# A gated transformer block on one core: a new hand-fixed order, with small operations shared out anew and thirteen more ordering pairs

## The chip, the cores and the metric

The kernel runs on one NeuronCore of one Trainium2 chip. The metric is the device time of one execution in microseconds (us). The engines are TensorE (PE: matmuls, and PEld: the weight loads that overlap them), VectorE (DVE), ScalarE (ACT), GpSimd (POOL) and SyncE (SP), which issues nearly all DMA transfers. Each engine works through its own instruction list strictly in order and waits on semaphores where an operand comes from another engine or from a transfer.

## The reference

One block on a sequence of 2048 tokens with 448 features, in bfloat16: attention in a sliding window and a gated MLP with a spatial product, each behind a layer norm that a conditioning vector modulates.

```python
mod = (silu(c) @ w_mod)                      # six vectors of 448
sa, ca, ga, sb, cb, gb = split(mod)
h = layernorm(x) * (1 + ca) + sa
x = x + ga * A(h)
h = layernorm(x) * (1 + cb) + sb
return x + gb * B(h)

def A(x):                                    # 16 heads of 28
    q, k, v = split(x @ wqkv)
    scores = q @ k.T * 28 ** -0.5
    scores = where(0 <= i - j < 256, scores, -1e9)
    return (softmax(scores) @ v) @ wo

def B(x):                                    # w_in: 448 x 1792
    z = gelu(x @ w_in)
    z1, z2 = z[:, :896], layernorm(z[:, 896:])
    return (z1 * (w_sp @ z2 + b_sp)) @ w_out # w_sp: 2048 x 2048
```

## The kernel before

The kernel is built in two passes. First every operation is recorded with `add`: the engines that may run it, its dependencies, and the buffers or PSUM banks (`take`) that it needs. Each gets a number in the order of recording. Then `order()` walks the words of a string, `ORDER`. A word such as `188.p.0.2` says: operation 188 goes next on PE (p; a is ACT, v DVE, g GpSimd, s SP) and takes options 0 and 2 of its buffers. So the string fixes at once which engine runs an operation, the order within each engine, and which buffers are reused when; a reused buffer adds a dependency on its last readers. A second string, `AFTER`, holds pairs such as `54-368`: operation 368 is to wait for operation 54 as well. `count`, `waits` and `emit` then turn dependencies into semaphore waits and leave out those that an engine's earlier waits already cover. The times that `order()` works out along the way steer nothing here.

The work in the program, in the order of time:

- Start: x comes in as two half blocks (L371: 256 tokens each, 224 KB) and three blocks of 512 tokens (L362, 448 KB each). w_mod and wqkv come in by pieces (L357, L358, L367, L368), wqkv's first into a staging tile `wq_st`, from which small copies (L543, L544) spread the heads into `WQK`. TensorE runs warm-up matmuls (L509) whose results nobody reads.
- Each tile of 128 tokens gets its statistics on DVE (L552, L555, L557, L564; L560 on GpSimd), a norm into `xn` (L572 on DVE, L579 on GpSimd), a transpose on TensorE and an evacuation with the modulation into `hT` (L637 on ACT, L639 on DVE).
- q and k come from `hT` and `WQK` and are evacuated 256 wide (L704 on ACT, L705 on DVE) or 512 wide (L725 on ACT, L726 on DVE) into `qT` and `KT`; v is evacuated into `Vaug` (L756, L757).
- Attention: scores (L827, TensorE), exps on ScalarE straight from PSUM into `PA` (L860 for the main blocks, L892 for the strips beside them), mask products on DVE or GpSimd (L870, L907, L910), weighted sums (L936), the output projection (L959).
- The second norm and `hT`, then z = h @ w_in: the second half z2 by tokens (L1015), with gelu on ScalarE (L1026, L1038), squares for its variance (L1047) and the normalisation on DVE (L1033, L1052) or GpSimd (L1030); the first half z1 by features (L1061).
- The spatial product (L1085) in two halves `wspA` and `wspB` of w_sp, which DMA transposes (L432) bring in transposed; b_sp and the gate (L1089, L1092); the last product (L1104) and the outputs.

Of the kernel before, what the change touches and what calls it, by code (L numbers as in the profile page):

```python
# [22 lines left out]
AFTER = "54-368 469-468 460-563 393-291 447-336 384-282 523-811 329-328 160-49 281-284 401-291 418-129 410-127 414-331 426-431 511-614 510-814 515-811 666-682 822-820 385-284 289-291 821-820"  # L23
# [50 lines left out]
class Sched:  # L74
# [23 lines left out]
    def order(self):  # L98
# [3 lines left out]
        self.prog = {e: [] for e in ENGS}  # L102
        for pair in AFTER.split():
            first, then = pair.split("-")
# [1084 lines left out]
```

## Time and profile before

| what | value |
|---|---|
| time, median of 3 runs | 269.0 us (268.57 to 269.16) |
| the profiled execution's own time | 268.23 us |
| its span in the trace | 266.5 us |
| instructions on PE / DVE / ACT / POOL | 2919 / 358 / 189 / 181 |
| granted TensorE clock | 1.00 throughout |
| HBM read and written | 9.53 MB and 1.84 MB |

The span is that of the one execution which the profiler followed, and 1.73 us of that execution's time lie outside it. The busy time of TensorE in the table of engines includes warm-up matmuls. The share of busy time is an average over stages that have different limits, so the profile is read by stage: the start up to the first exp at 15.97 us, attention up to about 99, z up to 146.07, where the spatial product starts, and from there to the end.

### The profile page before, as it was taken

The numbers are of one execution on the slowest core, as the hardware profiler recorded it, in microseconds if no ns is written. First come the engines' busy times: TensorE is split into PE (matmuls) and PEld (weight loads), VectorE is DVE, ScalarE is ACT, GpSimd is POOL, SyncE is SP. The second block draws the span as 40 slices with busy tenths as digits, with TensorE's granted clock in tenths as the row PEclk, the third lists the DMA queues.
The fourth block names the chain that finished last, engine by engine and source line by source line (L and its number), as shares of the span: only waits on it lengthen the run. The fifth ranks groups of instructions, "written<-read, shape, count | busy, mean of one in ns | idle before, by whom it ended". The sixth has DMA issues, their size and how long they took to land.

```text
span 266.5 us, 6861 instructions
## 1 busy us (share of the span) xinstructions
PE 261.0 (98%) x2919; PEld 136.3 (51%) x2919; DVE 152.5 (57%) x358; ACT 131.0 (49%) x189; POOL 132.6 (50%) x181
## 2 busy tenths in 40 slices
PE   7999999999999999999999999999999999999996
PEld 3764565565577666454444444444444444444454
DVE  6799999999999998887363001112203242033264
ACT  3799899999999995779996400000000000000000
POOL 7656665556599666452876002315604845030430
PEclk9999999999999999999999999999999999999999
DMA  7990425982996646449999994000000000000133
GB/s 221 331 326 16 99 40 81 126 106 44 165 207 81 126 80 91 82 98 183 180 175 194 170 195 114 0 2 0 1 0 2 0 0 0 2 17 0 52 114 95
DMA packets 66297, 25.46 MB, mean 96 GB/s; under 512 B 57813, under 2 KB 65562, under 8 KB 66266
## 3 DMA queue, kind: packets, MB, share of 16 engines
q1 hardware_dynamic: 65848, 24.52, 46.0%
q8 instruction: 23, 0.38, 0.6%
q10 hardware_dynamic: 418, 0.50, 0.5%
q14 instruction: 8, 0.07, 0.1%
HBM read 9.53 MB, written 1.84 MB: 43 GB/s over the span
## 4 chain that ended last, share of the span: by engine, by line
PE 88%; ACT 8%; DVE 2%; POOL 1%; issue 0%; ACTq 0%
PE ps L1085 36%; PE ps L1015 8%; PE ps L1061 8%; PE ps L1104 8%; PE ps L715 5%; ACT PA L860 5%; PE ps L827 5%; PE ps L936 4%; PE ps L752 4%; PE ps L959 3%; PE ps L679 2%; ACT PA L892 2%; PE ps L509 2%; POOL PA L870 1%; POOL rs_all L560 1%; DVE PA L910 0%
## 5 line engine op out<-in xcount | busy, mean ns | idle before, releaser
L1092 POOL TENSOR_TENSOR z1T<-tmpg,z1T 128x512 bf16<-128x512 bf16 x28 | 31.9, 1154 | 73.7 <-DVE tmpg L1089 73.7
L1089 DVE TENSOR_TENSOR tmpg<-ps,bsp_bc 128x512 bf16<-128x512 f32 x28 | 18.8, 689 | 86.7 <-PE ps L1085 59.7
L860 ACT ACTIVATE PA<-ps 128x1536 bf16<-128x1536 f32 (+4 forms) x64 | 60.0, 974 | 1.1 <-PE ps L827 0.4
L1085 PE MATMUL ps<-wspB,z 128*128 128x512 bf16 x224 | 49.8, 379 | 0.0
L1085 PE MATMUL ps<-wspA,z 128*128 128x512 bf16 x224 | 49.3, 379 | 0.0
L1085 PEld LDWEIGHTS ps<-wspA,z 128*128 128x128 bf16 x224 | 21.8, 98 | 26.6 <-issue 0.4
L1085 PEld LDWEIGHTS ps<-wspB,z 128*128 128x128 bf16 x224 | 21.9, 98 | 26.3 <-DVE tmpg L1089 0.2
L936 PEld LDWEIGHTS ps<-Vaug,PA 128*128 128x128 bf16 x720 | 20.9, 96 | 5.2 <-issue 1.6
L560 POOL TENSOR_TENSOR rs_all<-ve_all,neghalf 128x1 f32<-128x1 f32 (+1 forms) x31 | 20.7, 678 | 4.1 <-DVE ve_all L557 3.7
L1015 PE MATMUL ps<-w_in,hT 64*128 64x448 bf16 x224 | 22.7, 349 | 0.0
L936 PE MATMUL ps<-Vaug,PA 128*128 128x32 bf16 x720 | 22.5, 176 | 0.0
L1061 PE MATMUL ps<-hT,w_in 64*128 64x512 bf16 x196 | 22.3, 376 | 0.0
L1104 PE MATMUL ps<-w_out_g,z1T 128*128 128x448 bf16 (+3 forms) x126 | 22.2, 332 | 0.0
L870 POOL TENSOR_TENSOR PA<-PA,mask 128x1024 bf16<-128x1024 bf16 x7 | 15.9, 2274 | 8.5 <-ACT PA L860 2.9
L715 PE MATMUL ps<-hT,WQK 128*128 128x512 bf16 x80 | 20.0, 380 | 0.0
L827 PE MATMUL ps<-qT,KT 32*64 32x64 bf16 (+3 forms) x768 | 18.0, 223 | 1.4 <-ACT PA L860 0.6
L552 DVE BATCH_NORM_STATS2 st_all<-x_sb 128x6 f32<-128x448 bf16 x32 | 19.2, 612 | 0.0
L579 POOL TENSOR_SCALAR xn<-x_sb,rs_all,ve_all 128x448 bf16<-128x448 bf16 x18 | 14.8, 828 | 6.1 <-DVE PA L907 2.1
L892 ACT ACTIVATE PA<-ps 128x1536 bf16<-128x1536 f32 (+1 forms) x16 | 16.4, 1024 | 2.2 <-PE ps L827 2.0
L907 DVE TENSOR_TENSOR PA<-PA,mask 128x2048 bf16<-128x2048 bf16 x14 | 16.9, 1216 | 0.5 <-ACT PA L860 0.3
L1104 PEld LDWEIGHTS ps<-w_out_g,z1T 128*128 128x128 bf16 x126 | 11.7, 98 | 10.1 <-DVE fin L1115 0.2
L1015 PEld LDWEIGHTS ps<-w_in,hT 64*128 64x128 bf16 x224 | 10.8, 94 | 10.7 <-issue 0.4
(114 smaller groups left out, 334.0 us busy)
## 6 DMA issues: line engine op xcount, KB each, us to landing
w_in<-in_B_w_in_dram SPq DMA_DIRECT2D x8, 224.0 KB, 4.0
out_dram<-fin SPq DMA_DIRECT2D x15, 112.0 KB, 1.7
x_sb<-in_A_x_dram SPq DMA_DIRECT2D x3, 448.0 KB, 4.4
wmod<-in_w_mod_dram SPq DMA_DIRECT2D x1, 1344.0 KB, 9.6
w_out_g<-in_B_w_out_dram SPq DMA_DIRECT2D x1, 784.0 KB, 6.2
wq_st<-in_A_wqkv_dram SPq DMA_DIRECT2D x3, 224.0 KB, 4.6
bsp_bc<-in_B_b_sp_dram SPq DMA_DIRECT2D x1, 512.0 KB, 5.1
x_sb<-in_A_x_dram SPq DMA_DIRECT2D x2, 224.0 KB, 3.6
```

The lines of the kernel that those rows point to most:

```text
L552: st = [dve(0.62 if True else 0, lambda e, t=t, ci=ci, s=s: e.bn_stats(st_all[:, slot, t, ci, :], s()), deps(t), prio) for ci, s in enumer ...
L560: rs = pool(0.41 + 0.155 * len(tiles), lambda e: e.tensor_tensor(rs_all[:, slot, a:b], ve_all[:, slot, a:b], neghalf[:, 0:b - a], ALU.pow) ...
L715: m = pe(4 * MMS, [lambda e, h=h, g=g, kc=kc, tb=tb: e.matmul(ps[:, h.slot[0], :], lhsT=WQK[:, kc, 4 * g:4 * g + 4, :].rearrange("p a b -> ...
L827: return [lambda e, t=t: e.matmul(to(t), lhsT=KT[32 * t:32 * t + 32, qi, key:key + kn], rhs=qT[32 * t:32 * t + 32, qi, q0:q0 + qn], start= ...
L860: return e.activation(cols(place(kb, hf) + 64 + 768 * a, [[384, 2 * (b - a)], [1, w]]), ps[:, h.slot[0]:h.slot[0] + b - a, 2 * n * w:(2 * ...
L892: return e.activation(cols(EXTRAS[ext[n].slot[0]] + 128 * a, [[128, b - a], [512, 4], [1, 128]]), ps[:, h.slot[0]:h.slot[0] + b - a, :].re ...
L936: fns.append(lambda e, hO=hO, hd=hd, bi=bi, kb=kb, nb=nb, j=j, c=(2 * t + k) * 384 + 128 * (j - kb), half=half: e.matmul(ps[:, hO.slot[0], ...
L1015: return lambda e, kc, p0, start, stop: e.matmul(ps[:, hs[t % 2].slot[hf], 0:D], lhsT=hT[p0:p0 + 64, kc, t * 128:(t + 1) * 128], rhs=w_in[ ...
L1061: return lambda e, kc, p0, start, stop: e.matmul(ps[:, hs[b // 2].slot[b % 2], :], lhsT=w_in[p0:p0 + 64, kc, ft * 128:(ft + 1) * 128], rhs ...
L1085: m = pe(16 * MMS, [lambda e, h=h, si=si, ft=ft, tb=tb: e.matmul(ps[:, h.slot[0], :], lhsT=z2[:, si, ft * 128:(ft + 1) * 128], rhs=(wspA i ...
L1092: u = pool(1.16, lambda e, ht=ht, ft=ft, tb=tb: e.tensor_tensor(z1T[tb][:, ft, :], tmpg[:, ht.slot[0], :], z1T[tb][:, ft, :], ALU.mult), [ ...
L1104: return [lambda e, ft=ft: e.matmul(ps[:, h.slot[0], c0:c1], lhsT=z1T[t // 4][:, ft, (t % 4) * 128:(t % 4 + 1) * 128], rhs=w_out_g[:, ft, ...
```

## The change

Only the two strings differ. `ORDER` names the same operations in another sequence and puts 84 of them on another engine: DVE has 367 recorded operations after 358, GpSimd 166 after 177, ScalarE 176 after 174; TensorE's 326 and SP's 127 stay the same in number. Small operations (memsets, copies, norms, evacuations) make up most of those that move. `AFTER` has 35 pairs after 22, and the 13 new ones stand at its end. The other pairs are kept.

```diff
 ORDER = """
-2.a 28.v 39.g 0.s 37.g 29.v 30.v 31.v 32.v 58.p.0 40.g 3.a 4.s 43.g ...
+2.a 28.v 37.g 0.s 30.v 35.v 43.g 65.p.0 3.a 4.s 32.v 73.p.0 39.g 67.p.0 ...
 """
-AFTER = "54-368 469-468 ... 289-291 821-820"
+AFTER = "54-368 469-468 ... 289-291 821-820 427-328 477-597 443-338 238-239 380-384 422-331 426-328 464-468 481-564 490-581 632-648 506-814 982-976"
```

The first place is SP's queue at the start. `x_sb` is x in SBUF, `wq_st` the staging tile of wqkv; `128x2x448` is half a block of x and `128x4x448` a whole one. Before, from the third load of SP's queue on:

```order
L368 DMA wq_st<-in_A_wqkv_dram 128x896
L371 DMA x_sb<-in_A_x_dram 128x2x448
L368 DMA wq_st<-in_A_wqkv_dram 128x896 x2
L367 DMA wq_st<-in_A_wqkv_dram 64x896
L362 DMA x_sb<-in_A_x_dram 128x4x448
L358 DMA wo_g<-in_A_wo_dram 64x448
L358 DMA wv<-in_A_wqkv_dram 64x448
L362 DMA x_sb<-in_A_x_dram 128x4x448
```

And after the change, from the same load on:

```order
L368 DMA wq_st<-in_A_wqkv_dram 128x896
L362 DMA x_sb<-in_A_x_dram 128x4x448
L371 DMA x_sb<-in_A_x_dram 128x2x448
L368 DMA wq_st<-in_A_wqkv_dram 128x896 x2
L367 DMA wq_st<-in_A_wqkv_dram 64x896
L362 DMA x_sb<-in_A_x_dram 128x4x448
L357 DMA wv<-in_A_wqkv_dram 128x3x448
L358 DMA wv<-in_A_wqkv_dram 64x448
L358 DMA wmod<-in_w_mod_dram 64x1792
L357 DMA wmod<-in_w_mod_dram 128x3x1792
L432 DMA_TRANSPOSE wspA<-in_B_w_sp_dram 128x1024
L358 DMA wo_g<-in_A_wo_dram 64x448
```

Block 2 of x, which stood as the second `128x4x448` of the first list, now stands ahead of the second half block and of three pieces of wqkv. Block 3, not shown, comes next after the last row, and so behind a DMA transpose of w_sp.

The second place is DVE between the first statistics of the second half block and the first `hT`. `mv_all` and `ve_all` are the means and variances; the `COPY` rows with `wq_st` spread wqkv. Before:

```order
L552 BN_STATS st_all<-x_sb 128x6
L543 COPY WQK<-wq_st 128x16x28
L555 BN_AGGR mv_all<-st_all 128x2
L557 TENSOR_SCALAR ve_all<-mv_all 128x1
L543 COPY WQK<-wq_st 128x16x28 x2
L564 SCALAR_TENSOR_TENSOR ve_all<-mv_all,rs_all 128x1
L449 MEMSET wv 64x224
L572 TENSOR_SCALAR xn<-x_sb,mv_all,rs_all 128x448 x2
L639 TENSOR_SCALAR hT<-ps,modT 128x256 x3
```

After:

```order
L552 BN_STATS st_all<-x_sb 128x6
L555 BN_AGGR mv_all<-st_all 128x2
L543 COPY WQK<-wq_st 128x16x28
L557 TENSOR_SCALAR ve_all<-mv_all 128x1
L543 COPY WQK<-wq_st 128x16x28
L564 SCALAR_TENSOR_TENSOR ve_all<-mv_all,rs_all 128x1
L543 COPY WQK<-wq_st 128x16x28
L572 TENSOR_SCALAR xn<-x_sb,mv_all,rs_all 128x448 x2
L552 BN_STATS st_all<-x_sb 128x6
L705 CAST qT<-ps 128x256
L639 TENSOR_SCALAR hT<-ps,modT 128x256 x2
```

The memset has left this place, the last copy stands behind the small `ve_all` step, and a statistics step and an evacuation of q have moved ahead of `hT`'s.

The third place is ScalarE from its first exp on: `PA` holds the exps, and the other rows are evacuations. Before:

```order
L892 ACTIVATE PA<-ps 128x3x4x128
L892 ACTIVATE PA<-ps 128x4x128
L860 ACTIVATE PA<-ps 128x6x256
L756 ACTIVATE Vaug<-ps 128x16x28
L860 ACTIVATE PA<-ps 128x2x256
L860 ACTIVATE PA<-ps 128x6x256
L704 ACTIVATE KT<-ps 128x256
L860 ACTIVATE PA<-ps 128x2x256
L860 ACTIVATE PA<-ps 128x6x256
```

After:

```order
L892 ACTIVATE PA<-ps 128x3x4x128
L892 ACTIVATE PA<-ps 128x4x128
L860 ACTIVATE PA<-ps 128x6x256
L860 ACTIVATE PA<-ps 128x2x256
L860 ACTIVATE PA<-ps 128x6x256
L756 ACTIVATE Vaug<-ps 128x16x28
L860 ACTIVATE PA<-ps 128x2x256
L860 ACTIVATE PA<-ps 128x6x256
L520 ACTIVATE gg_sb<-ps 128x448
L860 ACTIVATE PA<-ps 128x2x256
L860 ACTIVATE PA<-ps 128x6x256
L725 ACTIVATE qT<-ps 128x512
```

The Vaug evacuation stands later and the KT evacuation has gone to DVE; a 512-wide evacuation of q, which DVE did, has come in.

More of the change, by code (lines that the diff above doesn't have):

```diff
@@ L21 @@
 """
-AFTER = "54-368 469-468 460-563 393-291 447-336 384-282 523-811 329-328 160-49 281-284 401-291 418-129 410-127 414-331 426-431 511-614 510-814 515-811 666-682 822-820 385-284 289-291 821-820"
+AFTER = "54-368 469-468 460-563 393-291 447-336 384-282 523-811 329-328 160-49 281-284 401-291 418-129 410-127 414-331 426-431 511-614 510-814 515-811 666-682 822-820 385-284 289-291 821-820 427-328 477-597 443-338 238-239 380-384 422-331 426-328 464-468 481-564 490-581 632-648 506-814 982-976"
 class Hold:
```

2 lines of the change are left out of this document (1 added, 1 removed).

## The prediction

> **What bounds the kernel now.** I read the page's head and chain first, then busy time in six stretches, then who waits for whom from 15 to 100 us, then single rows.
>
> The first fence holds the head of the page with its chain by engine; then the busy times by stretch (stretch, its length, busy PE, PEld, DVE, ACT, POOL, the granted clock, the DMA share, GB/s); then two groups of the waits between 15 and 100 us (idle us, how many, the longest), and three links of the chain.
>
> ```profile
> span 266.5 us, 6861 instructions
> PE 261.0 (98%) x2919; PEld 136.3 (51%) x2919; DVE 152.5 (57%) x358; ACT 131.0 (49%) x189; POOL 132.6 (50%) x181
> PE 88%; ACT 8%; DVE 2%; POOL 1%; issue 0%; ACTq 0%
> 0.00:15.20 15.20, 13.57 (x121) 8.42 (x122) 11.52 (x39) 9.32 (x21) 9.60 (x25) 1.00 0.91 277
> 15.20:24.00 8.80, 8.29 (x155) 4.94 (x156) 8.31 (x26) 8.37 (x11) 6.80 (x8) 1.00 0.53 191
> 24.00:52.00 28.00, 27.94 (x519) 14.79 (x516) 26.46 (x52) 26.82 (x31) 17.32 (x16) 1.00 0.50 78
> 52.00:99.00 47.00, 46.08 (x1060) 29.65 (x1059) 46.16 (x93) 45.15 (x53) 32.62 (x46) 1.00 0.71 118
> 99.00:146.00 47.00, 47.00 (x509) 23.13 (x506) 31.97 (x106) 38.23 (x70) 29.41 (x55) 1.00 0.78 141
> 146.00:266.50 120.50, 118.09 (x576) 55.41 (x574) 28.13 (x46) 3.13 (x7) 36.81 (x34) 1.00 0.19 43
> PEld ps L827 <- ACT PA L860: 5.7, 15, 0.5
> ACT PA L892 <- PE ps L827: 2.0, 5, 0.7
> 73.91 1.46 ACT PA L860
> 77.36 1.95 ACT PA L860 x2
> 146.07 72.62 PE ps L1085 x336
> ```
>
> TensorE looks like the bound all along, but four regimes lie under its 98%. Up to 15.2 us the DMA is 91% busy: the kernel waits for its loads, and much of TensorE's work there is warm-up matmuls that nobody reads. From 15.2 to 99 TensorE lacks 0.51 + 0.06 + 0.92 = 1.49 us, ScalarE 0.43 + 1.18 + 1.85 = 3.46 and DVE 0.49 + 1.54 + 0.84 = 2.87: three engines full at once, and the chain hops onto ScalarE's exps (L860, L892), whose banks the next scores (L827) wait for. From 99 to 146 TensorE has no idle time at all, and from 146 it streams the spatial product. So a delay put on the first exp, or work added to ScalarE before 99, comes out at the end, less what of those 1.49 us it closes; a delay on GpSimd or DVE behind 99 must first be longer than its cover.
>
> **The start loads.** In SP's queue the 448 KB of x block 2 now stand ahead of the second half of x block 0 and of three pieces of wqkv. The rows are SP's issues (start, length), three landings (KB each, us from issue), the first consumers on DVE, and the first exp on ScalarE.
>
> ```profile
> 3.04 0.43 SPq L371 DMA_DIRECT2D x_sb<-in_A_x_dram  x1
> 3.51 0.94 SPq L368 DMA_DIRECT2D wq_st<-in_A_wqkv_dram  x2
> 4.50 0.47 SPq L367 DMA_DIRECT2D wq_st<-in_A_wqkv_dram  x1
> 6.42 0.38 SPq L362 DMA_DIRECT2D x_sb<-in_A_x_dram  x1
> 10.40 0.49 SPq L362 DMA_DIRECT2D x_sb<-in_A_x_dram  x1
> x_sb<-in_A_x_dram SPq DMA_DIRECT2D x1, 224.0 KB, 4.5
> wq_st<-in_A_wqkv_dram SPq DMA_DIRECT2D x1, 112.0 KB, 4.9
> x_sb<-in_A_x_dram SPq DMA_DIRECT2D x1, 448.0 KB, 4.2
> 7.55 0.63 DVE L552 BATCH_NORM_STATS2 st_all<-x_sb 128x6 f32<-128x448 bf16 x1
> 9.28 0.46 DVE L543 COPY WQK<-wq_st 128x448 bf16<-128x448 bf16 x2
> 9.90 0.24 DVE L449 MEMSET wv<- 64x224 uint32 x1
> 10.18 0.70 DVE L572 TENSOR_SCALAR xn<-x_sb,mv_all,rs_all 128x448 bf16<-128x448 bf16 x2
> 11.38 1.05 DVE L639 TENSOR_SCALAR hT<-ps,modT 128x256 bf16<-128x256 bf16 x3 [0.49 <-PE ps L630]
> 15.97 2.08 ACT L892 ACTIVATE PA<-ps 128x1536 bf16<-128x1536 f32 x2 [0.39 <-PE ps L827]
> ```
>
> The half block, issued at 3.04, lands 4.5 later, at 7.54; DVE's statistics start on it at 7.55. The last wqkv piece lands at 4.50 + 4.9 = 9.40, between the starts of the two copies (9.28 and about 9.5), so the second takes it as it lands; the norms and transposes that lead to the first exp at 15.97 follow without a hole. Loads land in the order of their issue. From 9.40 to the landing of x block 1 at 6.42 + 4.2 = 10.62, 448 KB took 1.2 us while the DMA was 91% busy. Put ahead, block 2 moves everything behind it by that 1.2; with its own issue on SP (0.38 to 0.59 for such loads) partly in front, I take 1.3. Bounds: 0 if other engines of the DMA were free for it, 1.8 if the issue adds in full. The 1.2 is a price of this very transfer at this very place, so I stay close to it.
>
> The Trainium skill's page "DMA: Bandwidth & Descriptors", section "Where 436 GB/s comes from", says that a load from HBM is bound by the core's share of HBM, about 358 GB/s, and not by the 435 of the ports; as estimates 1.28 or 1.05 us for 448 KB, and the term by the one or the other would be that. The rows' 1.2 us (about 380 GB/s) lies between, so this trace does not show the lower figure as a strict limit.
>
> Between statistics and norms a memset (L449, 0.24, with its step 0.28) leaves DVE: −0.25. Two of the warm-up groups that TensorE runs ahead of the modulation go later, but what follows waits for the same loads: 0. A statistics step (0.63) now stands ahead of `hT`'s evacuations, where DVE waited 0.49 for a transpose: 0, and with the small evacuation that comes along up to +0.4. First exp: 1.3 − 0.25 = +1.05.
>
> **ScalarE from 16 to 50 us.** Its rows here, and the mean of the 512-wide evacuation:
>
> ```profile
> 19.28 0.55 ACT L756 ACTIVATE Vaug<-ps 128x448 bf16<-128x448 f32 x1
> 21.51 0.43 ACT L704 ACTIVATE KT<-ps 128x256 bf16<-128x256 f32 x1
> 27.57 2.08 ACT L892 ACTIVATE PA<-ps 128x1536 bf16<-128x1536 f32 x2 [0.67 <-PE ps L827]
> L725 ACT ACTIVATE qT<-ps 128x512 bf16<-128x512 f32 x4 | 2.4, 596 | 0.0
> ```
>
> Between the first and the third main exp a Vaug evacuation (0.55) and a KT evacuation (0.43) leave and one Vaug evacuation (0.55) comes in: −0.43. After that two evacuations of about 0.59 leave and three of 0.60 come, one of them before the 0.67 us in which ScalarE waited at 27.57 for scores: net 1.80 − 1.18 = 0.62 added, 0.67 of it covered: 0. If the cover is gone because the scores are late too, +0.6; if the scores come early, −0.4. From about 50 us to 99 ScalarE's order is unchanged, so it carries its shift on.
>
> **DVE takes over small work.** Rows: GpSimd's and DVE's norm (count, sum, mean ns), and the norms on GpSimd that go over first.
>
> ```profile
> L579 POOL TENSOR_SCALAR xn<-x_sb,rs_all,ve_all 128x448 bf16<-128x448 bf16 x16 | 13.4, 842 | 5.7 <-DVE PA L907 2.1 <-DVE PA L870 1.5 <-DVE PA L910 1.3
> L572 DVE TENSOR_SCALAR xn<-x_sb,mv_all,rs_all 128x448 bf16<-128x448 bf16 x3 | 1.2, 388 | 0.0
> 17.11 2.82 POOL L579 TENSOR_SCALAR xn<-x_sb,rs_all,ve_all 128x448 bf16<-128x448 bf16 x4 [0.30 <-DVE ve_all L564]
> ```
>
> Between 15.2 and 24 three norms come over: 3 × 0.388 = 1.16 us more on an engine with 0.49 idle, so at most 0.67 of delay for the evacuations queued behind them. Each leaves GpSimd 0.84 sooner, which helps the same transposes. Bounds 0 and 0.7; most evacuations there are TensorE's feed one tile ahead, so I take +0.2, nearer to the lower end. Over 24 to 99 some further small operations come, against 2.4 us of idle time: 0, up to +0.5.
>
> The Trainium skill's page "SBUF — State Buffer", section "Who interferes with whom", speaks against such a move: DVE's scalar operations can use the port pair that it shares with GpSimd, and whichever engine issues first keeps the other out for its whole instruction. By it each of the three norms could stand behind one of GpSimd's (0.71), and the term would be up to 0.67 + 2.1; the 388 ns mean on DVE, with GpSimd at work through those stretches, shows no such wait. On GpSimd's side the trace agrees: the same norm takes 0.71 in the four at 17.11 and 0.84 in the mean, the rest of them beside DVE's mask products.
>
> **The seam and the end.** ScalarE's square, GpSimd's last normalized tile before the spatial product, and SP's last transposes of w_sp:
>
> ```profile
> 112.11 1.08 ACT L1047 ACTIVATE fin<-z,mv_all 128x896 bf16<-128x896 bf16 x1
> 143.99 1.09 POOL L1030 TENSOR_SCALAR z<-z,rs_all,ve_all 128x896 bf16<-128x896 bf16 x1
> 142.21 8.95 SPq L432 DMA_TRANSPOSE wspB<-in_B_w_sp_dram  x6
> ```
>
> One gelu that frees banks for the gate's matmuls now stands behind such a square, 1.08 later: the other banks' matmuls lie between, and TensorE has no idle time there to show how many, so +0.1, with bounds from 0 to half a square, 0.5. The last tile of z is ready at 145.08, the spatial product starts at 146.07: 1 us of slack, and the order there brings that tile no later. The last transposes for the first half stand two places sooner. Behind 146 the tables differ little: 0.
>
> **The sum.** 1.05 − 0.43 + 0 + 0.2 + 0.1 = +0.92. The profiled execution took 268.23 (span 266.5 and 1.73 around it), 0.77 under the median of 269.0. I put the shift on the median: 269.9. Its own bounds: start 0.8 to 1.5 in place of 1.05, ScalarE −0.4 to +0.6 about its term, DVE 0 to 0.7, seam 0 to 0.5, which do not all go one way; I take +0.4 to +2.5, 269.4 to 271.5.
>
> **Rivals.**
> Faster (0.22): the start's delay is absorbed. The loads of the early stage have spare places (wmod's large pieces land sooner or later without a reader), the memset and the two warm-up groups go, and the regrouped evacuations close TensorE's waits of 15 to 99 us. These hold 1.49 at most, and half of it with −0.43 and −0.25 is −1.4 at best: 267.6 to 268.4, at its middle 268.0. It decides if the first exp starts at 15.97 or sooner. For it: three engines have their waits at the same places, where small moves pay; against it: 7.55 and 9.40 are starts on the instant of a landing.
>
> Slower by far (0.13): x block 3 stands behind a DMA transpose of w_sp in SP's queue, and more transposes follow it early. It was issued at 10.40, and this row shows when it was first read:
>
> ```profile
> DMA to landing us min/median/max: 2.8/4.4/10.1
> 23.79 0.62 DVE L552 BATCH_NORM_STATS2 st_all<-x_sb 128x6 f32<-128x448 bf16 x1
> ```
>
> The longest landing, 10.1, is this load's: 20.5, so 3.3 us of cover. Transposes go at 8.95 / 6 = 1.5 us each; two of them ahead take 3 us and a third 4.5, and then DVE's in-order queue stands, and evacuations with it: +1 to +2 on top of the forecast, about 272. It decides once block 3 lands after 24.
>
> No change (0.13): block 2's transfer finds gaps (the DMA share is 91%, that is 1.4 us of 15.2 unused), the start loses only 0.3, and the other terms cancel: 268.9.
>
> **How the numbers follow.** Forecast 0.52, of which 0.06 lie within 0.2% (0.54 us, about what a measurement of this kernel can tell from no change). Faster 0.22; same 0.13 + 0.06 = 0.19; slower 0.46 + 0.13 = 0.59. The range leaves out about a tenth at each end: into the faster rival down to 268.2, up to the middle of the far slower one at 272.0.
>
> **What would show it.** In the changed kernel's profile: DVE's first statistics of the second half block at 8.7 to 8.9 in place of 7.55; the last wqkv copy at 10.6 to 10.8; the first L892 row at about 17.0; the ScalarE row at 73.91 about 0.8 later; the first L1085 row at about 147. A first L892 at 16.0 or below refutes the start; L1085 at 147 and an end that is not later by as much refutes the stream; a stall on DVE at L552 around 24 to 27 us is the far slower case.

## The result, and the profile after

The changed kernel took 270.41 us (median of 6 runs, 270.02 to 270.66) where the kernel before, run beside it, took 269.01: a ratio of 1.0051 with a 95% interval of 1.0038 to 1.0064, or +1.40 us. Run a second time on another occasion it took 270.88 beside 268.65, 1.0079 (1.0066 to 1.0092). Forecast were 269.9 and a range of 268.2 to 272.0.

The two traces differ by more than the medians, since the profiled execution of before was 0.77 below its median and that of after (270.52) 0.11 above: span 266.5 against 268.6, +2.1. A shift that is read against the trace of before can therefore be some tenths too large.

The head of the page after, with its chain by engine, and two groups of its waits between 15 and 100 us (idle us, how many, the longest):

```profile
span 268.6 us, 6839 instructions
PE 259.3 (97%) x2898; PEld 135.9 (51%) x2919; DVE 156.5 (58%) x367; ACT 132.1 (49%) x191; POOL 126.1 (47%) x170
PE 74%; ACT 10%; DVE 9%; DMA 2%; issue 1%; SPq 1%
PEld ps L827 <- ACT PA L860: 7.6, 19, 0.6
ACT PA L892 <- PE ps L827: 1.8, 5, 0.4
```

DVE's share of the chain went from 2% to 9%, and transfers are now in it. Where the 2.1 us came in is read by following the same rows down the two traces. SP's start, the first reader of the half block on DVE, and ScalarE's first exp, its next strip exp and the exp that stood at 52.44 before (its row of before is put last):

```profile
3.04 0.45 SPq L362 DMA_DIRECT2D x_sb<-in_A_x_dram  x1
3.53 0.51 SPq L371 DMA_DIRECT2D x_sb<-in_A_x_dram  x1
9.40 0.63 DVE L552 BATCH_NORM_STATS2 st_all<-x_sb 128x6 f32<-128x448 bf16 x1 [1.04 <-DMA x_sb<-in_A_x_dram]
17.61 2.08 ACT L892 ACTIVATE PA<-ps 128x1536 bf16<-128x1536 f32 x2 [0.39 <-PE ps L827]
28.89 2.08 ACT L892 ACTIVATE PA<-ps 128x1536 bf16<-128x1536 f32 x2 [0.29 <-PE ps L827]
53.67 2.08 ACT L892 ACTIVATE PA<-ps 128x1536 bf16<-128x1536 f32 x2 [0.44 <-PE ps L827]
...
52.44 2.08 ACT L892 ACTIVATE PA<-ps 128x1536 bf16<-128x1536 f32 x2 [0.30 <-PE ps L827]
```

The half block is read 1.85 later (9.40 for 7.55), the first exp stands 1.64 later (17.61 for 15.97), and by 53.67 ScalarE has won 0.41 of that back: +1.23. It keeps this until 75 us. Then DVE, GpSimd, TensorE and ScalarE show this (the last row is the kernel before):

```profile
74.06 1.64 DVE L564 SCALAR_TENSOR_TENSOR ve_all<-mv_all,rs_all 128x1 f32<-128x1 f32 x1
73.56 2.12 POOL L870 TENSOR_TENSOR PA<-PA,mask 128x1024 bf16<-128x1024 bf16 x1 [1.82 <-DVE PA L870]
77.01 0.40 PE L827 MATMUL ps<-qT,KT 32*128 32x256 bf16 x8 [0.43 <-DVE ve_all L564]
79.75 0.93 PE L959 MATMUL ps<-wo_g,hT 128*128 128x448 bf16 x4 [0.39 <-DVE ve_all L557]
77.46 4.05 ACT L860 ACTIVATE PA<-ps 128x1536 bf16<-128x1536 f32 x4 [0.34 <-PE ps L827]
81.82 1.45 ACT L860 ACTIVATE PA<-ps 128x1536 bf16<-128x1536 f32 x1 [0.31 <-PE ps L827]
148.35 10.74 PE ps L1085 x49
...
79.83 1.45 ACT L860 ACTIVATE PA<-ps 128x1536 bf16<-128x1536 f32 x1
```

A step on one column of numbers (L564), which takes 0.14 to 0.17 us in 14 of its 17 places in this trace, took 1.64 us: from 74.06 to 75.70, while GpSimd's mask product ran from 73.56 to 75.68. DVE's queue stood behind it, TensorE waited 0.43 and 0.39 for what DVE brought late, and ScalarE's exps after that are about 2.0 late (81.82 for 79.83). This step, operation 596, ran on GpSimd before. On the chain the spatial product begins at 148.35 for 146.07, and the span ends 2.1 later, so nothing more is added behind it.

### The profile page after: what moved, and what is told of

Read it like the earlier page. It is cut to its first block, busy times and chain, and to the rows that moved or that the text cites. A ratio compares the mean times of both kernels' runs of the same rounds, so it can differ in the third digit from the quotient of the medians.

```text
span 268.6 us, 6839 instructions
## 1 busy us (share of the span) xinstructions
PE 259.3 (97%) x2898; PEld 135.9 (51%) x2919; DVE 156.5 (58%) x367; ACT 132.1 (49%) x191; POOL 126.1 (47%) x170
## 4 chain that ended last, share of the span: by engine, by line
PE 74%; ACT 10%; DVE 9%; DMA 2%; issue 1%; SPq 1%
PE ps L1085 36%; PE ps L1015 8%; PE ps L1061 8%; PE ps L1104 8%; ACT PA L860 7%; PE ps L959 3%; PE ps L715 3%; PE ps L827 3%; PE ps L936 3%; ACT PA L892 3%; DMA wq_st<-in_A_wqkv_dram 2%; DVE st_all L552 2%; PE ps L752 2%; DVE PA L907 1%; DVE xn L572 1%
## 5 line engine op out<-in xcount | busy, mean ns | idle before, releaser
L860 ACT ACTIVATE PA<-ps 128x1536 bf16<-128x1536 f32 (+3 forms) x64 | 60.2, 974 | 1.8 <-PE ps L827 0.9
L1085 PE MATMUL ps<-wspB,z 128*128 128x512 bf16 x218 | 49.2, 379 | 0.3
L560 POOL TENSOR_TENSOR rs_all<-ve_all,neghalf 128x1 f32<-128x1 f32 (+1 forms) x31 | 19.8, 639 | 8.3 <-DVE ve_all L557 7.4
L870 POOL TENSOR_TENSOR PA<-PA,mask 128x1024 bf16<-128x1024 bf16 x8 | 18.0, 2247 | 7.3 <-ACT PA L860 3.8
L715 PE MATMUL ps<-hT,WQK 128*128 128x512 bf16 x71 | 17.8, 379 | 1.0 <-ACT PA L860 0.3
L1069 ACT ACTIVATE z1T<-ps 128x512 bf16<-128x512 f32 x28 | 14.8, 607 | 2.3 <-PE ps L1061 2.3
```

Of the source, the lines that this page charges most:

```text
L560: rs = pool(0.41 + 0.155 * len(tiles), lambda e: e.tensor_tensor(rs_all[:, slot, a:b], ve_all[:, slot, a:b], neghalf[:, 0:b - a], ALU.pow) ...
L715: m = pe(4 * MMS, [lambda e, h=h, g=g, kc=kc, tb=tb: e.matmul(ps[:, h.slot[0], :], lhsT=WQK[:, kc, 4 * g:4 * g + 4, :].rearrange("p a b -> ...
L860: return e.activation(cols(place(kb, hf) + 64 + 768 * a, [[384, 2 * (b - a)], [1, w]]), ps[:, h.slot[0]:h.slot[0] + b - a, 2 * n * w:(2 * ...
L1085: m = pe(16 * MMS, [lambda e, h=h, si=si, ft=ft, tb=tb: e.matmul(ps[:, h.slot[0], :], lhsT=z2[:, si, ft * 128:(ft + 1) * 128], rhs=(wspA i ...
```

## The experiments

Each edit moves words of `ORDER`; a number with v, g or s is one operation on DVE, GpSimd or SP. "Before" is always the kernel before, run on the same chip in the same job. The ratio is taken over the executions and need not be the quotient of the two medians.

| run | median us | before us | ratio (95%) | first exp in its trace |
|---|---|---|---|---|
| x2_back | 269.88 | 268.73 | 1.0047 (1.0035 to 1.0059) | 16.91 |
| x2_front | 269.92 | 268.73 | 1.0056 (1.0041 to 1.0071) | 17.45 |
| early_var | 269.89 | 268.73 | 1.0051 (1.0024 to 1.0077) | 17.43 |
| both_mended | 269.32 | 268.73 | 1.0026 (1.0012 to 1.0041) | 17.84 |
| start_whole | 269.95 | 268.65 | 1.0037 (1.0024 to 1.0050) | 16.86 |
| all_mended | 269.29 | 268.65 | 1.0024 (1.0014 to 1.0033) | 17.26 |
| changed_again | 270.88 | 268.65 | 1.0079 (1.0066 to 1.0092) | 17.77 |
| lock_in_before | 270.25 | 268.65 | 1.0059 (1.0043 to 1.0075) | 16.27 |
| start_full | 270.22 | 268.73 | 1.0057 (1.0043 to 1.0071) | 16.96 |
| all_full | 269.50 | 268.73 | 1.0026 (1.0010 to 1.0041) | 16.49 |
| best_try | 269.23 | 268.93 | 1.0012 (0.9997 to 1.0027) | 16.38 |

**The load alone, put into the kernel before.**

```diff
-... 6.s 41.g 62.p.0 47.g 1.s ... 11.s 150.v 73.p.4 163.a 188.p.0.2 164.p.3 15.s ...
+... 6.s 41.g 62.p.0 47.g 15.s 1.s ... 11.s 150.v 73.p.4 163.a 188.p.0.2 164.p.3 ...
```

> The kernel before with one word moved: x block 2's load goes ahead of the second half block, as in the changed kernel. Theory 1: the half block is read 1.8 later, at about 9.4, the first exp at 17.6 to 17.9, and the time rises by 1.5 to 1.9 to 270.5 to 270.9, more than the whole change cost, since the savings of the change on ScalarE are not in it. Theory 2: attention's waits take the delay up, and the time rises by at most 0.5.

DVE's first read of the half block, the first exp, and the exp that stood at 52.44:

```profile
8.82 0.63 DVE L552 BATCH_NORM_STATS2 st_all<-x_sb 128x6 f32<-128x448 bf16 x1 [1.50 <-DMA x_sb<-in_A_x_dram]
17.45 1.45 ACT L892 ACTIVATE PA<-ps 128x1536 bf16<-128x1536 f32 x1 [0.39 <-PE ps L827]
54.05 2.08 ACT L892 ACTIVATE PA<-ps 128x1536 bf16<-128x1536 f32 x2 [0.45 <-PE ps L827]
```

One moved load costs +1.19 us between the medians and, by the ratio of 1.0056 (1.0041 to 1.0071), +1.5 us: four of the six executions lie at 269.8 to 270.0, two at 270.8 to 270.9. Expected were 1.5 to 1.9, with the half block read 1.8 later. The trace shows the mechanism: read 1.27 later, first exp +1.48, and +1.61 at 54.05, so attention took up none of it. It is a control for the forecast's ScalarE term as well: in the order before the delay grows by 0.13 from 16 to 54 us, in the changed order it shrinks by 0.41.

**The load alone, taken back in the changed kernel.**

```diff
-... 15.s 52.a 70.p.1 44.g 68.p.1 139.v 1.s ... 12.s ...
+... 52.a 70.p.1 44.g 68.p.1 139.v 1.s ... 12.s 15.s ...
```

> The changed kernel with one word moved: x block 2's load goes back behind wqkv's pieces and x block 1, as before. Theory 1 (the start's delay reaches the end): the second half block is read at about 7.55 in place of 9.40, the first exp stands at 15.9 to 16.1 in place of 17.61, and the time falls by 1.2 to 1.6, to 268.8 to 269.2. Theory 2 (the start is absorbed, and the loss comes from GpSimd keeping DVE out of its port at 74 to 75.7 and what waits behind it): the exp moves but the end falls by at most 0.4, to 270.0 or more.

```profile
8.20 0.62 DVE L552 BATCH_NORM_STATS2 st_all<-x_sb 128x6 f32<-128x448 bf16 x1
11.82 0.63 DVE L552 BATCH_NORM_STATS2 st_all<-x_sb 128x6 f32<-128x448 bf16 x1 [0.56 <-DMA x_sb<-in_A_x_dram]
16.91 2.08 ACT L892 ACTIVATE PA<-ps 128x1536 bf16<-128x1536 f32 x2 [0.39 <-PE ps L827]
```

The time is 269.88, still 1.15 above the kernel before. The first exp came only 0.70 sooner, and neither theory had that. One reason stands in the second row: in the changed order a statistics step that reads block 2 stands ahead of the evacuations of `hT`, and with the load back behind block 1 DVE waited 0.56 there. The order was made for the early load. The edit had undone one part and made a wait of the other. The 0.70 is itself uncertain: both_mended, below, has the same start, and its first exp stands at 17.84.

**The reader taken back too.** Operation 272 goes behind the statistics of block 1.

```diff
-... 15.s ... 1.s ... 12.s ... 272.v ... 227.v ... 276.v ...
+... 1.s ... 12.s 15.s ... 227.v ... 272.v 276.v ...
```

> The changed kernel with x block 2's load back behind x block 1, and with the one statistics step that reads block 2 (it stood ahead of the evacuations of hT on DVE) put behind the four steps that read block 1. If the first try fell short because that step now waited for block 2 in DVE's queue (0.56 us at 11.82): no wait for block 2 on DVE before 15 us, the first exp at 15.6 to 16.2, and the time 1.3 to 1.8 below the changed kernel on the same chip. If instead the start's delay has another cause in the changed order: first exp still at 16.8 or later and no more than 0.7 gained.

```profile
8.12 0.16 DVE L500 COPY modT<-ps 128x4 f32<-128x4 f32 x1 [1.51 <-PE ps L488]
8.45 0.41 DVE L639 TENSOR_SCALAR hT<-ps,modT 128x256 bf16<-128x256 bf16 x1
8.77 0.62 DVE L552 BATCH_NORM_STATS2 st_all<-x_sb 128x6 f32<-128x448 bf16 x1
16.86 2.08 ACT L892 ACTIVATE PA<-ps 128x1536 bf16<-128x1536 f32 x2 [0.39 <-PE ps L827]
```

The wait for block 2 is gone, but the first exp stays at 16.86, as in the expectation's second branch. The time is 0.93 below that of the changed kernel run beside it (270.88, changed_again), between the two branches. The half block is read at 8.77 although nothing waits for the load any more; DVE is held by the modulation, which TensorE brings at 8.12 (7.28 in the kernel before), and by an evacuation that now stands ahead of the statistics. So a second delay lay behind the first, hidden by the late load. Its size here is partly chance: this execution took 271.07, 1.12 above the median, and with the same order ahead of it the modulation came at 7.54 in x2_back and 8.06 in changed_again.

**The start as a whole.** Statistics (150) ahead of the modulation's copies, and two warm-up groups later.

```diff
-... 59.p.0 ... 61.p.0 ... 55.p.0 ... 112.v 164.p.2 113.v 162.v ... 150.v ... 69.p.1 ...
+... 55.p.0 ... 150.v 112.v 164.p.2 113.v 162.v ... 69.p.1 59.p.1 61.p.1 ...
```

> The changed kernel with block 2's load and its reader put back as in the run before, and two things more: the statistics of the second half block stand ahead of the modulation's copies on DVE (before, they stood right behind them), and two of the seven warm-up groups that TensorE runs ahead of the modulation go behind it. If the changed order is fitted to a late half block and has a second delay behind the first (the statistics started 8.77 with the load there at 7.51, since DVE held the modulation, 8.12, and an evacuation ahead of it): the statistics start at 7.5 to 7.6, the first exp at 15.6 to 16.1, and the time falls by 0.6 to 1.2 below the run before, to 0 to 0.5 above the kernel before (the port's lock is still in it). If the delay behind the loads is a third thing: first exp still after 16.5.

This run settles less than it was made for. The statistics start on the landing, but that came late in the traced execution, at 7.94, and the first exp stood at 16.96, beyond the 16.5 that the expectation named for a third cause; the time, 270.22, is no lower than that of start_whole, where 0.6 to 1.2 less was expected. With the same start the next run (all_full) read the half block at 7.47 and had its first exp at 16.49:

```profile
7.94 0.63 DVE L552 BATCH_NORM_STATS2 st_all<-x_sb 128x6 f32<-128x448 bf16 x1 [1.33 <-DMA x_sb<-in_A_x_dram]
...
7.47 0.63 DVE L552 BATCH_NORM_STATS2 st_all<-x_sb 128x6 f32<-128x448 bf16 x1 [0.86 <-DMA x_sb<-in_A_x_dram]
```

In all_full the norms that follow start at 10.06, 0.12 sooner than in the kernel before (10.18), and yet the first exp is 0.52 later. The transposes of these norms stand at 11.47 on TensorE, for 10.94 before, right behind 13 matmuls for q and k. So what is left of the start's loss in all_full comes in on TensorE, between the norms and their transposes.

**The port's lock.** This is the stall at 74.06, laid to the port pair that DVE shares with GpSimd. The step moves three places ahead in DVE's queue, so that it comes before GpSimd's product:

```diff
-... 469.v ... 464.v ... 627.v 345.v 468.g ... 596.v ...
+... 469.v ... 596.v 464.v ... 627.v 345.v 468.g ...
```

> The changed kernel with one small step of DVE (the variance step of L564 that took 1.64 us at 74.06 beside GpSimd's mask product) moved four places ahead in DVE's queue, so that it comes before that product starts. Theory 2 (the lock counts): the step takes 0.15 to 0.2, the scores behind it come 0.4 to 0.8 sooner, and the time falls by 0.6 to 0.9, to 269.5 to 269.8. Theory 1 (the start alone counts): at most 0.2 less, 270.2 or more. If it is a wait for data and not the port, the step's length stays above 1 us or the wait moves to the next step.

The step's new row, two other steps that run beside the product, a second L564, and the product:

```profile
72.75 0.15 DVE L564 SCALAR_TENSOR_TENSOR ve_all<-mv_all,rs_all 128x1 f32<-128x1 f32 x1
74.08 0.61 DVE L552 BATCH_NORM_STATS2 st_all<-x_sb 128x6 f32<-128x448 bf16 x1
74.84 0.56 DVE L757 CAST Vaug<-ps 128x448 bf16<-128x448 f32 x1
75.32 0.40 DVE L564 SCALAR_TENSOR_TENSOR ve_all<-mv_all,rs_all 128x1 f32<-128x1 f32 x1
73.58 2.12 POOL L870 TENSOR_TENSOR PA<-PA,mask 128x1024 bf16<-128x1024 bf16 x1 [1.88 <-DVE PA L870]
```

The step takes 0.15 in place of 1.64. DVE's statistics (one input in SBUF) and its cast from PSUM run at full speed beside the same product; a second L564, with two inputs in SBUF, ends at 75.72, with the product (75.70). TensorE's waits of 0.43 and 0.39 are gone. In the trace the exps after it come 0.7 sooner relative to the first one (80.92 for 81.82, with the first exp 0.19 sooner).

All traces of the changed order agree on this. Between the exps that stood at 75.39 and 81.30 in the kernel before, the delay grows by 0.86 to 0.88 in the five that have the step beside the product (after, changed_again, x2_back, start_whole, start_full), and by nothing in the five that have it ahead (early_var, both_mended, all_mended, all_full, best_try).

In time this run alone says little, since its interval (1.0024 to 1.0077) holds the changed kernel's. The pairs that differ in this step alone go the same way: 269.88 to 269.32 and 269.95 to 269.29, 0.56 and 0.66 us between the medians, 0.56 and 0.35 by the ratios, whose intervals still overlap.

**The same lock, made in the kernel before.** Operation 596 goes from GpSimd to DVE, into the time of another mask product.

```diff
-... 349.v ... 596.g ...
+... 349.v 596.v ...
```

> The kernel before with one step moved: the same variance step (operation 596) goes from GpSimd, where it took 0.26, to DVE, behind the evacuation of KT at 76.57, while GpSimd is in its mask product (76.07 to 78.63). If the port is held for the whole of that product: the step takes 1 to 1.4 us, until the product ends, DVE's queue stands behind it, and the time rises by 0.3 to 1.3. If the 1.64 us of the changed kernel was a wait for data: the step takes 0.15 to 0.2 and the time stays within 0.3.

The step and GpSimd's product in this run, and the step in the kernel before:

```profile
77.67 1.48 DVE L564 SCALAR_TENSOR_TENSOR ve_all<-mv_all,rs_all 128x1 f32<-128x1 f32 x1
76.60 2.54 POOL L870 TENSOR_TENSOR PA<-PA,mask 128x1024 bf16<-128x1024 bf16 x1 [0.15 <-ACT PA L860]
...
78.73 0.26 POOL L567 TENSOR_SCALAR ve_all<-mv_all,rs_all 128x1 f32<-128x1 f32 x1
```

It ends at 79.15, with the product (79.14). One small step on the wrong engine costs 1.6 us between the medians (1.0043 to 1.0075), above the 0.3 to 1.3 expected. The trace gives the step less: the delay is 1.70 at the exp that stood at 84.18, but 0.30 were there from the first exp on and 0.54 at 75.39, ahead of the step, so its own part is 1.16.

**Both, and what comes next.** These runs join the edits shown: the load and the step (both_mended), the load with its reader and the step (all_mended), and none, for a second trace (changed_again).

```diff
-... 15.s ... 1.s ... 12.s ... 464.v ... 596.v ...
+... 1.s ... 12.s 15.s ... 596.v 464.v ...          both_mended; all_mended with 272.v 276.v too
```

> The changed kernel with both words moved: x block 2's load back, and the variance step ahead of GpSimd's mask product. If the two causes are separate and add up: 1.2 to 1.6 and 0.6 to 0.9 less, 267.9 to 268.6, below the kernel before by 0.4 to 1.1. If one covers the other: no lower than the better of the two alone.

> The same, and the variance step of DVE ahead of GpSimd's mask product. If start and port lock add up: 1.9 to 2.5 below the changed kernel, so 0.3 to 0.9 below the kernel before, whose ScalarE does more between 16 and 50 us. If the lock's gain is covered by the next wait: no better than the run with the start alone.

> The changed kernel as it is, for the same chip and a second trace. If its two losses are in its order and not chance: the first exp at 17.3 to 17.8, the variance step at 1.5 to 1.7 us beside GpSimd's mask product, 1.2 to 1.6 above the kernel before. If the start is chance: the first exp moves by over 0.5 from 17.61.

Beside the changed kernel (270.88), load and reader gain 0.93 us (start_whole), and 1.59 with the step (all_mended), where 1.9 to 2.5 were expected. both_mended was expected at 267.9 to 268.6 and took 269.32. The two versions leave a loss, 1.0026 and 1.0024: the port's part is about as expected, the start's far less, and moving the reader as well gains nothing that these two show. Operation 596 took 1.64 again in the second trace of the changed kernel, and the first exp stood at 17.77, so both losses belong to its order; its time, 2.23 above the kernel before, is more than the 1.2 to 1.6 expected. The mended runs fell short of the kernel before for a further reason, shown where TensorE comes to 99 us sooner (start_whole, with the SP rows behind it):

```profile
100.21 0.93 PE L959 MATMUL ps<-wo_g,hT 128*128 128x448 bf16 x4 [1.01 <-DMA hT<-o_sb]
92.31 1.20 SPq L432 DMA_TRANSPOSE hT<-o_sb  x1
...
94.33 1.05 SPq L396 DMA_DIRECT2D w_in<-in_B_w_in_dram  x2
95.43 1.19 SPq L432 DMA_TRANSPOSE hT<-o_sb  x1
```

The second row is the kernel before, the last two the changed one: the transpose of `o_sb` is issued 3.1 us later, behind two loads of w_in. In the changed kernel's own trace it is just hidden; TensorE waited 1.01, 0.48 and 0.37 for it in start_whole, all_mended and early_var.

**Toward a version that beats both.** First the two w_in loads behind that transpose (all_full), then, since TensorE waited for them there, ahead of all late transposes, and without the two warm-up groups (best_try).

```diff
-... 22.s ... 23.s ... 24.s ... 742.s ...
+... 22.s ... 742.s 23.s 24.s ...          all_full
+... 22.s 23.s 24.s ... 742.s ...          best_try, without 59 and 61
```

> The same, with the variance step ahead of GpSimd's mask product, and two loads of w_in (224 KB each) behind the o_sb transpose for which TensorE waited 0.5 to 1.0 at 99 to 100 us where the run came there sooner. If these three are the losses of the changed kernel: no wait of TensorE above 0.3 at 99 us, 0.4 to 1.0 below the kernel before, at 267.7 to 268.3 on a chip where that takes 268.7. If the gains end in a wait that stands in both kernels: within 0.3 of the kernel before.

> The run before with its two new waits taken out: the two w_in loads go ahead of the late transposes, behind the w_in load at about 85 us, in place of behind them (there TensorE waited 0.63 for them at 100.30), and the two warm-up groups are left out in place of standing in front of the second transposes at 9.4. If the losses of the changed kernel are the start, the port's lock and the o_sb transpose: first exp at 15.9 to 16.3, no wait for a transfer above 0.2 between 98 and 102, and 0.2 to 0.8 below the kernel before. If what is left lies in many small places of the changed order: no lower than 0.3 above the kernel before.

all_full's new wait, and best_try's first exp:

```profile
100.30 1.88 PE L1015 MATMUL ps<-w_in,hT 64*128 64x448 bf16 x18 [0.63 <-DMA w_in<-in_B_w_in_dram]
...
16.38 2.08 ACT L892 ACTIVATE PA<-ps 128x1536 bf16<-128x1536 f32 x2 [0.39 <-PE ps L827]
```

all_full took 269.50, where 267.7 to 268.3 were expected. best_try stands at 1.0012 (0.9997 to 1.0027): the loss is down to what cannot be told from zero, but the kernel before is not beaten. By the medians it is 0.30 above, at the edge of the second branch, where 0.2 to 0.8 below were expected. Its first exp is still 0.4 behind. No engine waits for a transfer at 98 to 102 us any more, but DVE now waits 0.48 for a transpose of `o_sb` at 89.08, and the exps fall another 0.37 behind between 92 and 95; whether the one makes the other is not shown.

## Why the prediction was right, and where its steps were not

**The sum came out low, inside a wide range.** Forecast were +0.92 us; measured were +1.40 and +2.23. In the traces the terms are 1.64 for the start, −0.41 for ScalarE and about +0.8 for DVE, 2.1 in all, of which some tenths belong to the fast execution that the trace of before shows. The signs named came, each later than named: the half block at 9.40 for 8.7 to 8.9, the first exp at 17.61 for 17.0, the spatial product at 148.35 for 147.

**The direction and the place of the main term were right.** The load put ahead delays the second half block, that delays the first exp, and the delay reaches the end: shown by x2_front. The term was mis-sized in the changed kernel: 1.3 forecast, 1.85 at the half block, 1.64 at the first exp in place of 1.05; put into the kernel before it was 1.27 and 1.48. Two more traces with the changed start, changed_again and early_var, read the half block at 9.06 and 8.99 (1.51 and 1.44 later) and have their first exp at 17.77 and 17.43, and the start of the kernel before, unchanged in lock_in_before, put the first exp at 16.27. So 1.85 is the largest of three, and the term lies about between the 1.3 taken and the 1.8 named as upper bound. The memset's −0.25 came as forecast: from the statistics to the norms it is 2.42 (9.40 to 11.82) for 2.63.

**"Waits for the same loads: 0" hid a second delay, and its premise is a misreading.** The prediction has two warm-up groups go behind the modulation. In the changed `ORDER` 12 of them stand ahead of the modulation's first matmuls (operation 55), where 10 stood, and TensorE comes to these at 6.36 for 5.88. DVE gets the modulation at 7.62 for 7.28; over all traces it is 7.54 to 8.33 with the changed start's warm-up groups, 7.09 to 7.62 with those of the kernel before. An evacuation ahead of the statistics adds to it. In all_full, with two groups moved behind, TensorE ends the modulation's matmuls at 7.03, for 8.08 in start_whole. Beside the late load all this cost nothing, since DVE still waited 1.04 for the load; once the load was back, the half block was read at 8.20 and 8.77.

**ScalarE's term was right in total, not in its path.** Forecast were −0.43 for 16 to 50 us; −0.41 was found at 53.67, and x2_front, in the order before, has the reversed sign. But the forecast had all of it between the first and the third main exp, where the delay against the kernel before only goes from 1.71 to 1.42, and start_whole, with the same ScalarE order, gains 0.10 from its first exp to 54 us. So the agreement to 0.02 is in part luck.

**DVE's term was too small and stood in the wrong place.** Forecast were +0.2, with bounds of 0 and 0.7, at 15 to 24 us; found was about +0.8 in the trace at 75 to 82, and 0.56 to 0.66 between the medians of the pairs. The step that failed is the dismissal of the rule: the prediction weighed the Trainium skill's page "SBUF — State Buffer", section "Who interferes with whom", by the 388 ns of a norm (L572), and concluded that no such wait occurs. Those 388 ns were no test. They are the mean of three norms, at 25.00, 31.10 and 49.26, and GpSimd worked beside the last alone, for 0.07 us. The same section of the Trainium skill says that a DVE instruction with two inputs in SBUF contends with a GpSimd instruction that reads SBUF, since its second input comes through the shared read interface, and that this is an exclusive lock in which the issue order decides who blocks. The small variance step has two such inputs, and here the trace agrees: it ends within 0.02 us of GpSimd's product (75.70 and 75.68; 79.15 and 79.14). Of the small steps that the change moved, this is the one behind whose stall TensorE's waits follow.

The kernel before already shows such a stall, and the changed kernel shows that a single tensor input does not make a step safe. First come L564 and GpSimd's L536 before, then normalisations of z on DVE and on GpSimd after:

```profile
46.31 0.69 DVE L564 SCALAR_TENSOR_TENSOR ve_all<-mv_all,rs_all 128x4 f32<-128x4 f32 x1
45.95 1.04 POOL L536 TENSOR_TENSOR wo_g<-wo_g,gg_sb 128x448 bf16<-128x448 bf16 x1
...
141.68 0.51 DVE L1052 TENSOR_SCALAR z<-z,mv_all,rs_all 128x896 bf16<-128x896 bf16 x1
144.44 1.30 DVE L1052 TENSOR_SCALAR z<-z,mv_all,rs_all 128x896 bf16<-128x896 bf16 x1 [1.68 <-POOL rs_all L1051]
145.66 1.28 DVE L1033 TENSOR_SCALAR z<-z,mv_all,rs_all 128x896 bf16<-128x896 bf16 x1
144.41 2.29 POOL L1030 TENSOR_SCALAR z<-z,rs_all,ve_all 128x896 bf16<-128x896 bf16 x2
```

L564 took 0.69 and ended at 47.00, L536 at 46.99. The normalisations on DVE take 0.51 at 141.68 but 1.30 and 1.28 beside GpSimd's; they end at 146.94, ahead of the spatial product, so this costs nothing here. Not every GpSimd instruction holds DVE up: at 11.47 in the changed kernel L564 took 0.15, while GpSimd's L560, on one column, ran from 11.45 to 12.04.

**The seam's +0.1 is too small to be told here:** the delay is 2.08 at 86 us and 2.1 at the end.

**The rivals.** The faster one is refuted by the first exp at 17.61, no change by the interval of 1.0038 to 1.0064. The far slower one is refuted too: x block 3 was issued at 16.02, behind a transpose that held SP's queue for 4.50 us, but it was read at 26.07 without a wait:

```profile
10.00 4.50 SPq L432 DMA_TRANSPOSE wspA<-in_B_w_sp_dram  x1
16.02 0.59 SPq L362 DMA_DIRECT2D x_sb<-in_A_x_dram  x1
26.07 0.62 DVE L552 BATCH_NORM_STATS2 st_all<-x_sb 128x6 f32<-128x448 bf16 x1
```

What stays open: the last 0.3 us of best_try (within its interval); how much of the changed kernel's start is TensorE's order and how much DVE's, since start_full moved words of both and met a late landing; and why the changed kernel lay at +1.40 on one occasion and at +2.23 on the other. Which of the 13 added pairs matter was not tried one by one (`AFTER` has 36 pairs after 23).

## What to carry to other kernels

Before small steps go from GpSimd to DVE, ask of each which operands it has in SBUF and what GpSimd runs at that moment: a 0.15 us step behind a 2.1 us product stopped DVE's whole queue for 1.6 us. Look in the trace of before for small steps that end together with a GpSimd instruction; a mean over steps that never met one tells nothing. A transfer put ahead in a full queue delayed what follows by its full length here (about 1.2 us) and more, 1.3 to 1.9 us at the first reader, so price it there. And an order is fitted to itself: undoing one word of it shows the waits that stood behind, so a cause is measured best by putting it alone into the kernel before.

## What had not been expected of the hardware

The landing of a start load varies between executions. With the same start the half block was read on landing at 7.47 in one trace (all_full) and 7.94 in another (start_full). x2_back and both_mended have the same start too; the step that reads block 2 waited 0.56 in the one and 1.07 in the other, and their first exps stand at 16.91 and 17.84:

```profile
12.75 0.63 DVE L552 BATCH_NORM_STATS2 st_all<-x_sb 128x6 f32<-128x448 bf16 x1 [1.07 <-DMA x_sb<-in_A_x_dram]
```

These 0.93 us are most of the term under study. One trace can therefore not size a start; the medians and a second trace have to stand beside it.
